# Linformer attention and a maxout feed-forward on one core: swapping the halves of odd head pairs, and an ln moved ahead

## The chip, the core and the metric

The kernel runs on one core of a Trainium2 chip. The metric is the device time in microseconds of one execution. The engines of the core are named here as in the profile: PE is TensorE (its matmuls; PEld is its loading of weights, the stationary operand), DVE is VectorE, ACT is ScalarE, POOL is GpSimd, SP is SyncE. Matmuls write to PSUM, which the program holds as one tile `ps` of 128 partitions by 8 banks of 512 float32.

## The reference

```python
batch, n_heads, seq, head_dim, k_proj = 8, 8, 1024, 64, 64
k_proj = einsum('ks,bhsd->bhkd', E, k)            # 1024 keys become 64
v_proj = einsum('ks,bhsd->bhkd', F, v)
scores = q @ k_proj.T / sqrt(64)                  # 1024 x 64 for each head
attn   = exp(scores - max) / (sum + 1e-9)
x      = (attn @ v_proj) as [8192 tokens, 512]    # heads side by side
h      = maximum(maximum(x @ w1, x @ w2), x @ w3) # 512 -> 768
out    = h @ w_out                                # 768 -> 512
```

The weights are random with a standard deviation of 1/sqrt(fan-in), q, k and v of 0.1. The kernel computes in bf16 with float32 sums, and leaves out the maximum in the softmax.

## The kernel before

A batch goes through two stages: attention, which ends in the transposed activations `xT`, and the feed-forward in two halves of 512 tokens (`ch`): layer 1 (18 groups of four matmuls, `l1`) and the output projection (`down`). The attention of batch b+1 is sewn into the feed-forward of batch b: `tick()` counts groups, and `at(slot, ...)` puts a piece of attention behind the group with that number. [...]

Batch 0 has nothing to hide behind and is written in a form of its own. Eight heads make four pairs `g`, and the two heads of a pair are its halves `u`. In the scores of batch 0 a pair holds its projected keys on 128 partitions, 64 for each half, and the probabilities `pT` also have one half on partitions 0 to 63 and the other on 64 to 127:

```python
HEAD = (0, 1, 2, 3, 5, 4, 7, 6)
QUADS = [(hh, j, HEAD[4 * hh + j] // 2, HEAD[4 * hh + j] % 2) for j in range(4) for hh in range(2)]
AB = 4
HD = D // 2
# ...
def quads0(ch, bank, lhs, hhs=(0, 1)):
    for hh, j, g, u in QUADS:
        if hh not in hhs:
            continue
        rows = slice(u * KP, (u + 1) * KP)
        nc.tensor.matmul(out=ps[j * HD:(j + 1) * HD, bank + hh, :], lhsT=lhs(rows, g),
                         rhs=pT[0][rows, g, ch, :], start=True, stop=True, tile_position=(u * KP, j * HD))
# ...
def v_proj0(g, bank):
    for si in range(SI):
        for u in range(2):
            nc.tensor.matmul(out=ps[u * KP:(u + 1) * KP, bank, g * D:(g + 1) * D], lhsT=fT[:, si, :],
                             rhs=v_t[0][:, HEAD[2 * g + u], si, :], start=(si == 0), stop=(si == SI - 1))
    nc.vector.tensor_copy(out=vp2[0][:, g], in_=ps[:, bank, g * D:(g + 1) * D].rearrange("p (dd f) -> p f dd", f=2))

def scores0(ch, g, bank):
    for u in range(2):
        rows = slice(u * D, (u + 1) * D)
        nc.tensor.matmul(out=ps[u * KP:(u + 1) * KP, bank, :], lhsT=kpT[0][rows, g, 0, :],
                         rhs=qT[0][rows, 4 * ch + g, :], start=True, stop=True)
# ...
def scores_up0():                       # the second half of batch 0's tokens
    for g, bank in ((0, 4), (1, 5), (2, 6), (3, 7)):
        scores0(1, g, bank)
    for g in (0, 2):
        nc.scalar.activation(out=pT[0][:, g:g + 2, 1, :], in_=ps[:, 4 + g:6 + g, :], func=AF.Exp, scale=scale)
```

`quads0` serves for the sums (with ones as weights) and for the AV product (with the projected v): eight matmuls of 64 rows by 32 columns, in eight tiles of the array. A score matmul contracts 64 rows into 64 columns, so the array has four tiles for it: row half by column half. In the first half of the tokens the scores of the four pairs have other matmuls between them (`k_proj0`, `q_turn0`, warm-ups); only `scores_up0` has the four pairs one after the other.

For the later batches, sums, ln, reciprocal and AV are:

```python
def sums(b):
    for ch in range(2):
        quads(b, ch, AB + 2 * ch, lambda rows, g: ones[rows, :])
    log(0)

def log(ch):
    nc.scalar.activation(out=lns[ch], in_=ps[:, AB + 2 * ch:AB + 2 * ch + 2, :], func=AF.Ln)

def recip(ch):
    nc.scalar.activation(out=rinv[ch], in_=lns[ch], func=AF.Exp, scale=-1.0)
# ...
def norm(b, f, ch, bank):
    nc.vector.tensor_tensor(out=xT[b % 2][:, f::2, ch, :], in0=ps[:, bank:bank + 2, :],
                            in1=rinv[ch].rearrange("p (u n) -> p u n", u=2), op=ALU.mult)

def av3(b):
    lo = fpair()                        # a free pair of banks 0 to 3
    for f, ch, bank in ((0, 0, lo), (1, 0, AB), (0, 1, AB + 2)):
        av(b, f, ch, bank)
    norm(b, 0, 0, lo)
```

Each `av` is a set of eight matmuls as in `quads0`. The first of the three in `av3` goes to a pair of the feed-forward's banks, the second over the sums of the first half (banks 4, 5), the third over the sums of the second half (6, 7).

Where batch 1's attention lies in batch 0's feed-forward, and the same pieces of batch 2 in batch 1's:

```python
if b == 0:
    at(9, scores_up0)
    at(12, sums0, 1, 4)
    at(19, kv, 1)                       # projections of batch 1, need its k and v
    # ...
    at(27, scores, 1, 0)
    at(30, scores, 1, 1)
    at(33, sums, 1)
    at(34, recip, 0)
    at(35, log, 1)
    at(35, av3, 1)
    at(36, recip, 1)
    at(36, norm, 1, 1, 0, AB)
    at(38, norm, 1, 0, 1, AB + 2)
elif b == 1:
    at(2, kv, 2)
    # ...
    at(15, av1, 1)
    at(15, sums, 2)
    at(15, log, 1)
    at(16, recip, 0)
    at(18, recip, 1)
    # ...
    at(25, av3, 2)
```

`down(b, ch, c, tt)`, the output projection of 128 tokens, is six matmuls and a copy by ScalarE to `o_acc`; four of them end batch 0.

Of the kernel before, what the change touches and what calls it, by code (L numbers as in the profile page):

```python
# [16 lines left out]
def kernel(ctx: ExitStack, tc: tile.TileContext, q, k, v, E, F, w1, w2, w3, w_out, out):  # L17
    nc = tc.nc
    B, H, S, D = q.shape
    KP = E.shape[0]  # L20
# [11 lines left out]
    def T(shape, dt, name):  # L32
        return sb.tile(shape, dt, name=name)

    ps = pp.tile([P, 8, 512], FP32, name="ps")
# [6 lines left out]
    fT = T([P, SI, KP], BF16, "fT")  # L42
# [9 lines left out]
    kpT = [T([P, H, 2, KP], BF16, f"kpT{i}") for i in range(NB)]  # L52
    vp2 = [T([P, NPAIR, 2, D // 2], BF16, f"vp2_{i}") for i in range(3)]
    pT = [T([P, NPAIR, 2, 512], BF16, f"pT{i}") for i in range(2)]
# [59 lines left out]
    HD = D // 2  # L114

    def kv(b, bank=AB):
        i = b % NB
        for si in range(SI):
            nc.tensor.matmul(out=ps[0:KP, bank, :], lhsT=eT[:, si, :], rhs=k_t[i][:, :, si, :],  # L119
                             start=(si == 0), stop=(si == SI - 1))  # L120
            nc.tensor.matmul(out=ps[KP:P, bank, :], lhsT=fT[:, si, :], rhs=v_t[i][:, :, si, :],  # L121
                             start=(si == 0), stop=(si == SI - 1))
        kp_ = kp2[i].rearrange("k h f r dd -> k (h f) r dd")
        kv_v = ps[KP:P, bank, :].rearrange("p (g u dd f) -> p u g f dd", u=2, f=2, dd=HD)
        nc.scalar.copy(out=kp2[i][:, :, :, 0, :], in_=ps[0:KP, bank, :].rearrange("p (h dd f) -> p h f dd", dd=HD, f=2))  # L125
        nc.scalar.copy(out=vp2[b % 3][KP:P], in_=kv_v[:, 1])
        nc.vector.tensor_copy(out=kp_[:, :, 1:], in_=kp_[:, :, 0:1].to_broadcast([KP, 2 * H, 3, HD]))
        nc.vector.tensor_copy(out=vp2[b % 3][0:KP], in_=kv_v[:, 0])
        nc.sync.dma_start_transpose(out=kpT[i].rearrange("p h f k -> p (h f) k"),
                                    in_=kp2[i].rearrange("k h f r dd -> k (h f r dd)"))  # L130
# [60 lines left out]
    def fbank():  # L191
        ring.append(ring.pop(0))
        return ring[-1]
# [57 lines left out]
                nc.gpsimd.dma_start(out=out_0[0][:, tt - 1:tt + 1, :], in_=o_acc[0][:, tt - 1:tt + 1, :])  # L251


    def quads0(ch, bank, lhs, hhs=(0, 1)):
        for hh, j, g, u in QUADS:
            if hh not in hhs:
                continue
            rows = slice(u * KP, (u + 1) * KP)
            nc.tensor.matmul(out=ps[j * HD:(j + 1) * HD, bank + hh, :], lhsT=lhs(rows, g),  # L259
                             rhs=pT[0][rows, g, ch, :], start=True, stop=True, tile_position=(u * KP, j * HD))  # L260

    def k_proj0(g):
        for si in range(SI):
# [5 lines left out]
    def v_proj0(g, bank):  # L269
        for si in range(SI):  # L270
            for u in range(2):
                nc.tensor.matmul(out=ps[u * KP:(u + 1) * KP, bank, g * D:(g + 1) * D], lhsT=fT[:, si, :],
                                 rhs=v_t[0][:, HEAD[2 * g + u], si, :], start=(si == 0), stop=(si == SI - 1))
        nc.vector.tensor_copy(out=vp2[0][:, g], in_=ps[:, bank, g * D:(g + 1) * D].rearrange("p (dd f) -> p f dd", f=2))

    def scores0(ch, g, bank):
        for u in range(2):
            rows = slice(u * D, (u + 1) * D)
            nc.tensor.matmul(out=ps[u * KP:(u + 1) * KP, bank, :], lhsT=kpT[0][rows, g, 0, :],  # L279
                             rhs=qT[0][rows, 4 * ch + g, :], start=True, stop=True)  # L280

    def exp0(ch, g, bank):
# [36 lines left out]
    def av_up0():  # L319
        for f, bank in enumerate((6, 4)):  # L320
            quads0(1, bank, lambda rows, g: vp2[0][rows, g, f, :])
        norm0(1, 0, 6, (0, 1))
        norm0(1, 1, 4, (0, 1))
# [40 lines left out]
    for y, dst in enumerate((eT, fT)):  # L364
        for si in range(SI):
            for x in range(2):
                nc.tensor.matmul(out=ps[x * D:(x + 1) * D, y, si * KP:(si + 1) * KP], lhsT=ef_b[:, y, si::SI],
                                 rhs=ident[:, x::2], start=True, stop=True)
# [51 lines left out]
    def l1_first(i, jts, banks, between=None):  # L420
        for hh in range(2):
            if hh and between:
                between()
            for jt, bank in zip(jts, banks):
                for ct in (2 * hh, 2 * hh + 1):
                    nc.tensor.matmul(out=ps[:, bank, :], lhsT=w_sb[i][:, ct, jt * P:(jt + 1) * P], rhs=xT[0][:, ct, 0, :],  # L426
                                     start=(ct == 0), stop=(ct == NCT - 1))
                if hh:
                    nc.vector.tensor_tensor(out=h1c[jt] if i == 1 else hT[0][:, jt, :], in0=ps[:, bank, :], in1=h1c[jt],  # L429
                                            op=ALU.max)  # L430
                    yield
# [7 lines left out]
    load(1, v, v_t)  # L439
    load(1, q, q_t)  # L440
    v_proj0(0, 3)
    warmup(1, 2)
    sums_part0(1)
    warmup(4, 2)
    v_proj0(1, 3)
    warmup(1, 2)
    av0(0, 0)
    av0(1, 0)
    norm0(0, 0, 6, (0,))
    norm0(0, 1, 7, (0,))  # L450
    v_proj0(2, 3)
    warmup(1, 2)
    w1_ct(0)
# [13 lines left out]
    for b in range(B):  # L467
        n = b + 1
        groups = []

        def at(slot, f, *args):
            groups.append((slot, lambda: f(*args)))
# [4 lines that stand above are left out]
            at(19, kv, 1)  # L477
            for g, x in enumerate((21, 22, 24, 25)):
                at(x, q_flip, 1, g)
            at(22, load_behind_turn, 2, "kvq")  # L480
            at(27, scores, 1, 0)
            at(30, scores, 1, 1)
            at(33, sums, 1)
            at(34, recip, 0)
            at(35, log, 1)
            at(35, av3, 1)
            at(36, recip, 1)
            at(36, norm, 1, 1, 0, AB)
# [3 lines that stand above are left out]
            for g in range(4):  # L492
                at(4 + g, q_flip, 2, g)
            at(9, load_behind_turn, 3, "kvq")
            at(8, scores, 2, 0)
            at(12, scores, 2, 1)
# [5 lines that stand above are left out]
            at(24, load, 4, k, k_t)  # L502
            at(24, load, 4, v, v_t)
            at(25, av3, 2)
            at(26, norm, 2, 1, 0, AB)
            at(28, norm, 2, 0, 1, AB + 2)
            at(30, kv, 3)
            for g in range(4):
                at(32 + 2 * g, q_flip, 3, g)
        elif n < B:  # L510
            if b + 2 < B:
                at(3, lambda: kv(b + 2, fbank()))
            at(3, scores, n, 0)
            at(8, scores, n, 1)
            if b + 3 < B:
                at(11, load_behind_turn, b + 3, "qkv", 4 if b == 2 else None)
            at(14, av1, b)
            at(14, sums, n)
            at(14, log, 1)
            at(15, recip, 0)  # L520
            at(17, recip, 1)
            at(26, av3, n)
            at(27, norm, n, 1, 0, AB)
            at(29, norm, n, 0, 1, AB + 2)
            if b + 2 < B:
                for g in range(4):
                    at(33 + 2 * g, q_flip, b + 2, g)
        else:
            at(5, av1, b)
        slot = 0  # L530
        gi = 0

        def tick():
            nonlocal slot, gi
            slot += 1
            while gi < len(groups) and groups[gi][0] <= slot:
                groups[gi][1]()
                gi += 1

        for ch in range(2):  # L540
            c = 2 * b + ch
            if c == 0:
                for part in ((1, range(6), (6, 7, 0, 1, 4, 5)), (2, range(3), (2, 3, 0), q_up0), (2, range(3, 6), (1, 2, 3))):
                    for _ in l1_first(*part):
                        tick()
                ring[:] = [0, 1, 2, 3]
                for x in range(2):
                    if x:
                        av_up0()
                    for tt in range(4):  # L550
                        down_half(tt, x)
                        if x:
                            tick()
                continue
            for s in range(18):
                l1(b, ch, c, s // 3, s % 3)
                tick()
                if pend and s in (2, 5, 8, 11):
                    pend.pop(0)()
                    tick()  # L560
            pend = [lambda tt=tt, b=b, ch=ch, c=c: down(b, ch, c, tt) for tt in range(4)]
        if b == 0:
            while pend:
                pend.pop(0)()
                tick()
# [32 lines left out]
```

The softmax here doesn't subtract the row's maximum and nothing guards it: scores larger than these inputs give would overflow.

## Time and profile before

The device time is 397.1 us, the median of three runs (397.05 to 397.64). The profiled execution has a span of 395.6 us.

| | busy us | share of the span | instructions |
|---|---|---|---|
| TensorE matmuls | 385.5 | 97% | 2691 |
| TensorE weight loads | 173.6 | 44% | 2742 |
| VectorE | 201.0 | 51% | 296 |
| ScalarE | 162.7 | 41% | 247 |
| GpSimd | 66.5 | 17% | 109 |

How to read what follows: a timeline line has the start in us from the span's start, the length in us of what is merged in it, the engine, the line of the kernel, the operation, what it writes and reads, the shape, and how many instructions it holds (x8). In brackets at its end stands how long the engine was idle before it, and what released it. Matmuls are pipelined, and the end of one is modelled; starts are the safer figure. Some matmul records can be missing. A group of the page has busy time, mean ns of one instruction, and idle time before it. "The chain" is followed back from the last instruction, at each step to what released it.

Line numbers are those of the kernel before: L259 is the matmul in `quads0`, L279 in `scores0`, L155 in `quads` (sums and AV of the later batches), L141 in the later batches' scores, L119 and L121 in `kv`, L164 is ln, L167 the reciprocal, L173 the normalization, L208 layer 1, L233 and L235 `down`'s matmul and copy, L426 and L246 layer 1 and output projection of batch 0's first half, L87 the loads of q, k and v.

### The profile page before, as it was taken

Reading aid. Unit: us, or ns where it says so; the run is one execution under the profiler, and the core shown is the slowest. Engines: PE = TensorE matmul, PEld = TensorE weight load, DVE = VectorE, ACT = ScalarE, POOL = GpSimd, SP = SyncE. Lnnn points to the kernel's source line nnn. Section 1 sums busy time; section 2 is a strip of 40 time slices with the busy share of each in tenths; the row PEclk is TensorE's granted clock in tenths of the full one; section 3 lists DMA queues with packets and bytes.
Section 4 is the critical chain, followed back from the end, with each engine's and each line's share of the span. In section 5 each row is a group of like instructions: output and inputs, shape, how many; then the busy total and the mean of one; then the engine's idle time right before and its main releaser. Section 6 shows DMA issues by size and latency. Waiting matters only on the chain.

```text
span 395.6 us, 6594 instructions
## 1 busy us (share of the span) xinstructions
PE 385.5 (97%) x2691; PEld 173.6 (44%) x2742; DVE 201.0 (51%) x296; ACT 162.7 (41%) x247; POOL 66.5 (17%) x109
## 2 busy tenths in 40 slices
PE   8999998999999999999999999999999999999996
PEld 4444443444444444444444444444444444444443
DVE  3347375555662476435764347625664456443342
ACT  4414446465326613356224632266234452222221
POOL 7452131162002501050000500000010000000000
PEclk9999999999999999999999999999999999999999
DMA  8999979979953995169711893121011111101023
GB/s 224 206 209 206 205 178 202 224 117 205 206 139 81 174 206 168 42 119 204 180 56 28 152 205 123 55 59 64 13 53 55 53 56 53 56 36 70 2 106 106
DMA packets 41437, 48.39 MB, mean 122 GB/s; under 512 B 9152, under 2 KB 36544, under 8 KB 41408
## 3 DMA queue, kind: packets, MB, share of 16 engines
q0 software_dynamic: 31776, 43.52, 53.0%
q1 hardware_dynamic: 8656, 3.41, 4.6%
q10 hardware_dynamic: 976, 1.05, 0.8%
q8 instruction: 21, 0.34, 0.3%
q14 instruction: 8, 0.07, 0.0%
HBM read 57.15 MB, written 16.78 MB: 187 GB/s over the span
## 4 chain that ended last, share of the span: by engine, by line
PE 92%; DMA 5%; issue 1%; DVE 1%; ACT 0%; POOL 0%; POOLq 0%; DVEq 0%
PE ps L208 59%; PE ps L233 19%; PE ps L119 3%; PE ps L155 3%; DMA w_sb<-in_moe_w_dram 3%; PE ps L426 2%; PE ps L141 2%; DMA k_t<-in_k_dram 2%; PE ps L246 1%; PE ps L417 1%; PE ps L226 1%; PE ps L259 0%; DVE h1s L429 0%; DVE o_acc L429 0%; PE ps L279 0%
## 5 line engine op out<-in xcount | busy, mean ns | idle before, releaser
L208 PE MATMUL ps<-xT,w_sb 128*128 128x512 bf16 x1049 | 242.9, 379 | 1.7
L208 PEld LDWEIGHTS <-w_sb 128*128 128x128 bf16 x1080 | 103.6, 98 | 130.0 <-issue 8.6
L213 DVE TENSOR_TENSOR m<-ps,h1s 128x512 f32<-128x512 f32 x90 | 62.2, 691 | 131.5 <-PE ps L208 99.1
L233 PE MATMUL ps<-wo_sb,hT 128*128 128x512 bf16 x335 | 82.3, 379 | 0.5 <-issue 0.2
L211 ACT COPY h1s<-ps 128x512 f32<-128x512 f32 x90 | 53.0, 589 | 67.4 <-PE ps L208 67.0
L235 ACT COPY o_acc<-ps 128x512 f32<-128x512 f32 x58 | 34.0, 587 | 102.3 <-PE ps L233 86.8
L215 DVE TENSOR_TENSOR hT<-ps,m 128x512 bf16<-128x512 f32 x90 | 62.0, 689 | 10.2 <-PE ps L208 2.4
L240 POOL DMA_DIRECT2D out_dram<-o_acc x28 | 15.2, 543 | 265.9 <-ACT o_acc L235 263.7
L233 PEld LDWEIGHTS <-hT 128*128 128x128 bf16 x348 | 33.5, 98 | 41.2 <-issue 1.7
L173 DVE TENSOR_TENSOR xT<-ps,rinv 128x1024 bf16<-128x1024 f32 x28 | 33.5, 1218 | 10.0 <-PE ps L155 7.8
L146 ACT ACTIVATE pT<-ps 128x1024 bf16<-128x1024 f32 x28 | 27.1, 1021 | 6.5 <-PE ps L141 6.2
L101 DVE STREAM_TRANSPOSE qT<-q_t 128x512 f32<-128x512 f32 x28 | 18.6, 689 | 0.0
L87 POOL DMA_DIRECT2D v_t<-in_v_dram x21 | 15.3, 747 | 11.1 <-PE ps L208 4.7
L164 ACT ACTIVATE lns<-ps 128x1024 f32<-128x1024 f32 x14 | 13.7, 1022 | 5.8 <-PE ps L155 5.8
L167 ACT ACTIVATE rinv<-lns 128x1024 f32<-128x1024 f32 x14 | 14.8, 1062 | 0.0
L121 PE MATMUL ps<-v_t,fT 128*64 128x512 bf16 x56 | 13.4, 382 | 0.0
L119 PE MATMUL ps<-k_t,eT 128*64 128x512 bf16 x56 | 13.4, 382 | 0.0
L125 ACT CAST kp<-ps 64x512 bf16<-64x512 f32 x7 | 4.1, 579 | 18.5 <-PE ps L121 18.5
L87 POOL DMA_DIRECT2D k_t<-in_k_dram x14 | 10.6, 769 | 2.3 <-ACT o_acc L464 1.1
L87 POOL DMA_DIRECT2D q_t<-in_q_dram x14 | 10.6, 773 | 2.0 <-DMA wo_sb<-in_moe_w_out_dram 1.1
L426 PE MATMUL ps<-xT,w_sb 128*128 128x512 bf16 x46 | 10.6, 379 | 0.2 <-issue 0.2
L155 PE MATMUL ps<-pT,vp 64*32 64x512 bf16 x224 | 8.9, 381 | 1.8 <-ACT lns L164 1.0
(84 smaller groups left out, 159.2 us busy)
## 6 DMA issues: line engine op xcount, KB each, us to landing
out_dram<-o_acc POOLq DMA_DIRECT2D x30, 512.0 KB, 3.0
q_t<-in_q_dram POOLq DMA_DIRECT2D x15, 512.0 KB, 12.1
k_t<-in_k_dram POOLq DMA_DIRECT2D x14, 512.0 KB, 12.1
v_t<-in_v_dram POOLq DMA_DIRECT2D x18, 256.0 KB, 14.5
v_t<-in_v_dram POOLq DMA_DIRECT2D x7, 512.0 KB, 14.1
w_sb<-in_moe_w_dram POOLq DMA_DIRECT2D x4, 384.0 KB, 10.3
k_t<-in_k_dram POOLq DMA_DIRECT2D x4, 256.0 KB, 7.9
w_sb<-in_moe_w_dram POOLq DMA_DIRECT2D x4, 192.0 KB, 10.1
```

What stands on the lines that cost most here:

```text
L87: nc.gpsimd.dma_start(out=dst[b % NB][:, slots], in_=sv[:, heads])
L101: nc.vector.transpose(out=qT[b % NB][:, hs].bitcast(FP32).rearrange("p h n -> p (h n)"), in_=q_t[b % NB][:, hs].rearrange("p h si d -> p ( ...
L119: nc.tensor.matmul(out=ps[0:KP, bank, :], lhsT=eT[:, si, :], rhs=k_t[i][:, :, si, :], start=(si == 0), stop=(si == SI - 1))
L146: nc.scalar.activation(out=pT[i][:, 2 * u + gg].rearrange("p ch (t r n) -> p r (ch t) n", t=4, r=4), in_=ps[:, AB:AB + 4, gg * 256:(gg + 1 ...
L155: nc.tensor.matmul(out=ps[j * HD:(j + 1) * HD, bank + hh, :], lhsT=lhs(rows, g), rhs=pT[b % NB][rows, g, ch, :], start=True, stop=True, ti ...
L173: nc.vector.tensor_tensor(out=xT[b % 2][:, f::2, ch, :], in0=ps[:, bank:bank + 2, :], in1=rinv[ch].rearrange("p (u n) -> p u n", u=2), op= ...
L208: nc.tensor.matmul(out=ps[:, bank, :], lhsT=w_sb[i][:, ct, jt * P:(jt + 1) * P], rhs=xT[b % 2][:, ct, ch, :], start=(ct == 0), stop=(ct == ...
L211: nc.scalar.copy(out=h1s[jt % 2], in_=ps[:, bank, :])
L213: nc.vector.tensor_tensor(out=m12[jt % 2], in0=ps[:, bank, :], in1=h1s[jt % 2], op=ALU.max)
L215: nc.vector.tensor_tensor(out=hT[c % 2][:, jt, :], in0=ps[:, bank, :], in1=m12[jt % 2], op=ALU.max)
L233: nc.tensor.matmul(out=ps[:, bank, :], lhsT=hT[c % 2][:, jt, tt * P:(tt + 1) * P], rhs=wo_sb[:, jt, :], start=(jt == 0), stop=(jt == NJT - 1))
L235: nc.scalar.copy(out=o[:, tt, :], in_=ps[:, bank, :])
```

## The change

In batch 0 the halves of the odd pairs change places wherever they lie along the keys' axis: in the scores' output, in the projected v, and in what the sums and the AV product read. An even pair's scores then go from rows 0 to 63 to columns 0 to 63 and from rows 64 to 127 to columns 64 to 127 of the array, as before; an odd pair's go from the upper rows to the lower columns and the other way round. It is meant to let two pairs run side by side in all four 64x64 tiles. Apart from that, the second ln of batch 1 is put behind the first, ahead of the reciprocal and of the AV units that write over its sums. The number of instructions is the same on all engines, and so are the loads.

```diff
+    def half(g, u):
+        x = u ^ (g % 2)
+        return slice(x * KP, (x + 1) * KP)
+
     def quads0(ch, bank, lhs, hhs=(0, 1)):
         for hh, j, g, u in QUADS:
             if hh not in hhs:
                 continue
-            rows = slice(u * KP, (u + 1) * KP)
+            rows = half(g, u)
             nc.tensor.matmul(out=ps[j * HD:(j + 1) * HD, bank + hh, :], lhsT=lhs(rows, g),
-                             rhs=pT[0][rows, g, ch, :], start=True, stop=True, tile_position=(u * KP, j * HD))
+                             rhs=pT[0][rows, g, ch, :], start=True, stop=True, tile_position=(rows.start, j * HD))
 # ...
     def v_proj0(g, bank):
         for si in range(SI):
             for u in range(2):
-                nc.tensor.matmul(out=ps[u * KP:(u + 1) * KP, bank, g * D:(g + 1) * D], lhsT=fT[:, si, :],
+                nc.tensor.matmul(out=ps[half(g, u), bank, g * D:(g + 1) * D], lhsT=fT[:, si, :],
 # ...
     def scores0(ch, g, bank):
         for u in range(2):
             rows = slice(u * D, (u + 1) * D)
-            nc.tensor.matmul(out=ps[u * KP:(u + 1) * KP, bank, :], lhsT=kpT[0][rows, g, 0, :],
+            nc.tensor.matmul(out=ps[half(g, u), bank, :], lhsT=kpT[0][rows, g, 0, :],
                              rhs=qT[0][rows, 4 * ch + g, :], start=True, stop=True)
 # ...
             at(33, sums, 1)
+            at(33, log, 1)
             at(34, recip, 0)
-            at(35, log, 1)
             at(35, av3, 1)
```

## The prediction

> **What bounds the kernel now.** I read the page first: the engine totals, the slices and the chain that ended last.
>
> ```profile
> PE 385.5 (97%) x2691; PEld 173.6 (44%) x2742; DVE 201.0 (51%) x296; ACT 162.7 (41%) x247; POOL 66.5 (17%) x109
> ...
> PEclk9999999999999999999999999999999999999999
> ...
> PE 92%; DMA 5%; issue 1%; DVE 1%; ACT 0%; POOL 0%; POOLq 0%; DVEq 0%
> ```
>
> TensorE is busy 97% of a 395.6 us span at full granted clock, and 92% of the chain is its own work. So only two things shorten the run: less TensorE time, or an idle moment of TensorE taken away. The change offers one of each, and each is found in a narrow timeline.
>
> Part A is the upper half of batch 0's scores. These are TensorE's matmuls, then its weight load of what follows:
>
> ```profile
> 34.36 1.05 PE L279 MATMUL ps<-qT,kpT 64*64 64x512 bf16 x8
> 35.57 0.59 PE L426 MATMUL ps<-xT,w_sb 128*128 128x512 bf16 x2 [0.16 <-issue]
> ...
> 35.34 0.55 PEld L426 LDWEIGHTS <-w_sb 128*128 128x128 bf16 x4 [0.41 <-issue]
> ```
>
> Looked at in still narrower windows, the eight matmuls start two by two: at 34.36, 34.60, 34.82 and 35.04, some 0.22 us apart. That is four rounds of two. The last two starts are 0.30 us ahead of the next weight load at 35.34. The "0.16 issue" in front of the matmul at 35.57 isn't to be believed: the whole group has 12 weight loads (x12 at 35.34) and 11 matmul records (x11), so the first matmul's record is missing, and it ran with its load at 35.34. From the first score to the next block is therefore 35.34 - 34.36 = 0.98 us.
>
> Other small matmuls of the same kernel, in 64x32 tiles, show what more tiles at once give:
>
> ```profile
> 38.04 0.41 PE L259 MATMUL ps<-pT,ones 64*32 64x512 bf16 x8
> 38.38 0.39 PE L246 MATMUL ps<-wo_sb,hT 128*128 128x512 bf16 x1
> ...
> 41.08 0.63 PE L259 MATMUL ps<-pT,vp 64*32 64x512 bf16 x16
> 41.63 0.39 PE L246 MATMUL ps<-wo_sb,hT 128*128 128x512 bf16 x1
> ```
>
> Eight matmuls in eight tiles take 0.34 us until the next block starts; sixteen, two rounds, take 0.55. One round more costs 0.21.
>
> Part B is the end of batch 0, where batch 1's AV units run. TensorE and its weight load, then ScalarE:
>
> ```profile
> 65.17 0.62 PE L155 MATMUL ps<-pT,vp 64*32 64x512 bf16 x16
> 66.84 0.41 PE L155 MATMUL ps<-pT,vp 64*32 64x512 bf16 x8 [1.04 <-ACT lns L164]
> 67.17 0.33 PEld L233 LDWEIGHTS <-hT 128*128 128x128 bf16 x3 [0.23 <-issue]
> ...
> 62.83 1.02 ACT L164 ACTIVATE lns<-ps 128x1024 f32<-128x1024 f32 x1 [0.61 <-PE ps L155]
> 63.89 1.06 ACT L167 ACTIVATE rinv<-lns 128x1024 f32<-128x1024 f32 x1
> 65.28 0.59 ACT L235 COPY o_acc<-ps 128x512 f32<-128x512 f32 x1 [0.33 <-PE ps L233]
> 65.76 1.03 ACT L164 ACTIVATE lns<-ps 128x1024 f32<-128x1024 f32 x1
> ```
>
> The third AV unit writes the two banks that held the sums of the second half, so it has to wait until the second ln has read them. ScalarE does that ln fourth, after a reciprocal and a copy, although the sums were there at about 62.9. TensorE stands for 1.04 us. The same three units in batch 1, where both ln come before them:
>
> ```profile
> 97.47 0.84 PE L155 MATMUL ps<-pT,vp 64*32 64x512 bf16 x24
> 98.24 1.04 PE L233 MATMUL ps<-wo_sb,hT 128*128 128x512 bf16 x4
> ```
>
> **What the Trainium skill says.** "TensorE: Matmul & The Clock Gate", in "Part 3: Packing small matmuls — row/col tiling", says that matmuls in different tiles of the array run at the same time and start a few ns apart. The trace agrees: the pairs above start 3 ns apart. "TensorEngine Tiling (Array Packing)", "Restrictions and Gotchas", says that row tiles may not write one PSUM bank at the same moment. "PSUM — Partial Sum Buffer", in "PSUM bank collisions raise a hardware error", narrows that to the same quadrant of 32 partitions within a bank. The new layout keeps to it: even pairs fill the diagonal tiles, odd pairs the other two, and the two matmuls of one column half write different banks. "Perfetto Trace Analysis", "Tensor Engine Instruction (MATMUL, LD_WEIGHTS)", says that ScalarE is strictly first in, first out. That is what part B turns on, and the order above, with an ln behind a copy that itself waited 0.33 us, agrees.
>
> **The change part by part.**
>
> A. Nothing is added: the eight score matmuls are the same, but pairs 0 and 1 (then 2 and 3) now use four different 64x64 tiles. I count two rounds of four instead of four of two. Two rounds to the next block is the 0.55 us of the sixteen above, against 0.98: 0.43 us less. The start of batch 0 also calls the score function, but there other matmuls stand between the pairs, so nothing can overlap. The exp that follows (35.02 to 36.96) may start some 0.2 us earlier, and the sums that need it come at 38.04 - 0.43 = 37.61, still after it. Before the next block's second bank is free, VectorE must have finished its maximum, which runs from 34.21 to about 34.9; TensorE will want that bank at 34.91 + 0.43 = 35.34. So no new wait here.
>
> B. ScalarE's order becomes ln 0, ln 1, reciprocal 0, copy, copy, reciprocal 1. From the durations above, ln 1 ends about 62.83 + 2 x 1.02 = 64.87 at the latest, before AV starts at 65.17. The 24 matmuls then run in one piece as in batch 1: 98.24 - 97.47 = 0.77 us to the next block, where it now takes 67.17 - 65.17 = 2.00 us. That is 1.23 us less. Of it 1.04 is the wait shown; the rest is a pipeline that needn't start twice. (Here too I use the weight load at 67.17: 18 loads and 17 matmuls are recorded.)
>
> What B delays: reciprocal 0 ends about 65.93 instead of 64.95. The normalization on VectorE starts now at 65.72, so 0.2 us later; its two steps take 2.36 us and end near 68.3. The next layer-1 matmuls need them about 71.0 - 1.2 = 69.8. The copy of the first output tile ends about 66.5 instead of 65.9, and its bank is wanted by the third down block at about 65.94 + 1.29 = 67.2. Both have room.
>
> Sum: 0.43 + 1.23 = 1.66 us at most, if everything behind is TensorE's own. I checked what else has a date of its own. Batch 1's projection starts at 46.92, and v for it comes late:
>
> ```profile
> 31.16 0.72 POOL L87 DMA_DIRECT2D v_t<-in_v_dram  x1 [1.97 <-DMA q_t<-in_q_dram]
> ...
> v_t<-in_v_dram POOLq DMA_DIRECT2D x1, 256.0 KB, 15.3
> ...
> 46.92 0.40 PE L121 MATMUL ps<-v_t,fT 128*64 128x512 bf16 x1
> ```
>
> 31.16 + 15.3 is a landing near 46.5, and the DMA engines are full until about 53 us, so that date doesn't move with TensorE. After part A the projection would be ready at 46.49. That is exactly on the date; I take 0.07 us off for it. Batch 1's turned k lands at 55.13 (issue at 50.10, 5.0 us), its scores start at 55.78 - 0.36 = 55.42: room of 0.3. Batch 2's v lands about 69.1 for a projection at 72.89 - 1.6 = 71.3: room of 2. Later loads are earlier still against their use. So 1.6 us, of 397.1: 395.5.
>
> **Rivals.** First, v's date eats part A: if in an unprofiled run it lands 0.3 us later than in this one, A yields about 0.1, and the time is 395.8. For it: the near coincidence. Against: the kernel before shows no wait there at all.
>
> Second, four tiles don't run four at a time, say because two column halves can't take different moving data from the same rows. Then A is nothing and the time is 395.9. Against: the 64x32 matmuls above do this in eight tiles, and batch 1's scores put 32 matmuls of 256 columns into 0.59 us.
>
> Third, ScalarE's new order makes a wait elsewhere: a later reciprocal 0 holds up normalization, layer 1 and a bank. I put the room at 0.7 us or more; if it were none, B would keep about 0.9 and the time would be 395.8.
>
> Fourth, the swapped row order of the sums and AV units at the start (rows 0, 64, 64, 0 instead of alternating) costs a round. Until 20.8 us the chain is a weight transfer (10.27 to 20.50), which hides it; behind it a single pair of units is exposed, 0.2 us. The full sets already have neighbours on the same rows and run in one round, so I give this little.
>
> **Range and chances.** The best case is 397.1 - 1.7 = 395.4; with a run-to-run spread of 0.6 us in the three times before, 394.9 is the low end. If only B holds, and loses a few tenths, it is 396.2. Two per cent would be 7.9 us, almost five times what both parts hold, and nothing that is added could cost so much. So within 2% at 0.985, the rest for surprises.
>
> **What would show it.** The score line should read x8 with about 0.62 us instead of 1.05, and the next weight load come about 0.55 after it starts. On ScalarE the two ln should stand together near 62.4, before the first reciprocal; batch 1's AV should be one line of x24 with 0.84, without a wait for the ln. At the projection of batch 1 a wait for v of at most 0.1 us may appear; a longer one would speak for the first rival. The gap between the two traces should be 0.4 us at 36 us, 0.35 at 49 us, 1.6 at 70 us, and stay there. If it shrinks after 72 us, something with a date of its own has taken it back, and my reading of the later stages is wrong.

## The result

The changed kernel takes 395.85 us, the median of six runs (395.35 to 396.22), against 397.1 us in as many runs of the kernel before (397.05 to 397.92). The ratio is 0.9963, with a 95% interval of 0.995 to 0.9976: 1.5 us less by the ratio, with 1.0 to 2.0 in the interval; by the medians it is 1.25. The prediction was 395.5, in a range of 394.9 to 396.2.

The page of the kernel after, the same lines as were shown of the one before (in the second, of the chain, the order of the small shares differs):

```profile
PE 384.6 (98%) x2691; PEld 173.5 (44%) x2742; DVE 201.0 (51%) x296; ACT 162.5 (41%) x247; POOL 66.5 (17%) x109
...
PE 91%; DMA 6%; issue 1%; POOL 0%; ACT 0%; DVE 0%; POOLq 0%
```

TensorE is busier as a share of a span of 394.4 us, and a transfer has gained a place in the chain: the turned k of batch 2, below. From here on, lines of the kernel beyond `quads0` stand five further down: L279 has become L284, L426 L431.

Part A in the timeline after, matmuls and then weight loads:

```profile
34.05 0.63 PE L284 MATMUL ps<-qT,kpT 64*64 64x512 bf16 x8
34.83 2.54 PE L431 MATMUL ps<-xT,w_sb 128*128 128x512 bf16 x11 [0.16 <-issue]
...
34.60 1.41 PEld L431 LDWEIGHTS <-w_sb 128*128 128x128 bf16 x8 [0.41 <-issue]
```

From the first score to the next block's weight load it is 34.60 - 34.05 = 0.55 us, where it was 0.98. That is the predicted 0.43 us. The gap before the matmul at 34.83 is again a missing record: 12 matmuls are issued there and 11 recorded.

Part B: TensorE with its weight loads, then ScalarE, then VectorE:

```profile
64.46 0.84 PE L155 MATMUL ps<-pT,vp 64*32 64x512 bf16 x24
...
65.23 0.76 PEld L233 LDWEIGHTS <-hT 128*128 128x128 bf16 x5 [0.42 <-issue]
...
62.12 1.94 ACT L164 ACTIVATE lns<-ps 128x1024 f32<-128x1024 f32 x2 [0.61 <-PE ps L155]
63.95 1.06 ACT L167 ACTIVATE rinv<-lns 128x1024 f32<-128x1024 f32 x1
64.89 0.59 ACT L235 COPY o_acc<-ps 128x512 f32<-128x512 f32 x1
...
65.04 2.35 DVE L173 TENSOR_TENSOR xT<-ps,rinv 128x1024 bf16<-128x1024 f32 x2 [1.07 <-ACT rinv L167]
```

Both ln are through at 62.12 + 1.94 = 64.06, before the AV units start, and the 24 matmuls are one piece: 65.23 - 64.46 = 0.77 us instead of 2.00. Normalization now waits for the reciprocal, and no wait for normalization shows.

Then a part of it is lost. These are batch 2's first scores after and before, and the transfer that turns their k, which ScalarE's and VectorE's copies release. In this last view the number is the time from issue to landing:

```profile
79.76 0.66 PE L141 MATMUL ps<-qT,kpT 32*64 32x256 bf16 x32 [0.75 <-DMA kpT<-kp]
...
kpT<-kp SPq DMA_TRANSPOSE x1, 5.6
```

```profile
80.89 0.66 PE L141 MATMUL ps<-qT,kpT 32*64 32x256 bf16 x32
...
kpT<-kp SPq DMA_TRANSPOSE x1, 3.5
```

The turned k was issued at 74.12 instead of 76.07, and landed at 79.72 instead of 79.57. Set side by side, weight load by weight load, the kernel after is ahead by 0.31 us when it reaches the changed scores (the start of the two profiled runs differed by that), by 0.74 behind them, by 1.95 behind batch 1's AV units, and by only 1.13 from batch 2's scores to the end: 0.82 us lost on the turned k.

### The profile page after: what moved, and what is told of

It is laid out like the page before. It is cut to its first block, busy times and chain, and to the rows that moved or that the text cites. A ratio compares the mean times of both kernels' runs of the same rounds, so it can differ in the third digit from the quotient of the medians.

```text
span 394.4 us, 6594 instructions
## 1 busy us (share of the span) xinstructions
PE 384.6 (98%) x2691; PEld 173.5 (44%) x2742; DVE 201.0 (51%) x296; ACT 162.5 (41%) x247; POOL 66.5 (17%) x109
## 4 chain that ended last, share of the span: by engine, by line
PE 91%; DMA 6%; issue 1%; POOL 0%; ACT 0%; DVE 0%; POOLq 0%
PE ps L208 58%; PE ps L233 19%; PE ps L119 3%; PE ps L155 3%; PE ps L431 3%; DMA w_sb<-in_moe_w_dram 2%; PE ps L141 2%; DMA k_t<-in_k_dram 2%; DMA kpT<-kp 1%; PE ps L246 1%; PE ps L422 1%; PE ps L226 1%; PE ps L264 0%; PE ps L311 0%; POOL k_t L347 0%
## 5 line engine op out<-in xcount | busy, mean ns | idle before, releaser
L431 PE MATMUL ps<-xT,w_sb 128*128 128x512 bf16 x46 | 10.6, 379 | 0.2 <-issue 0.2
L127 DVE COPY kp<-kp 64x1536 bf16<-64x1536 bf16 x7 | 3.9, 552 | 12.4 <-ACT kp L125 12.4
```

## Experiments

The theory: A is worth 0.43 us, B 1.23, and what is missing is taken by a transfer with a date of its own. The rivals: a part is worth less away from the profile, or the late k was a single odd transfer. Leads are in us against the profiled kernel before, taken between the weight loads of both traces.

**Each part alone.** With the second ln back in its old place, and with the kernel before with that ln moved:

```diff
-            at(33, log, 1)
             at(34, recip, 0)
+            at(35, log, 1)
             at(35, av3, 1)
```

> The changed kernel with the second ln of batch 1 back where it was: part A alone. Theory (two rounds of four tiles, and batch 2's turned k has a date of its own): the eight score matmuls read 0.62 us instead of 1.05, 0.43 us are gained and pass to the end, because batch 2's scores then come at about 80.5 us and their k has landed by about 79.6: 396.7 us. Rival (the score matmuls gain nothing off the profile, the start is only scattered): 397.1.

> The kernel before with both ln ahead of batch 1's AV units: part B alone. Theory: AV runs as one line of 24 and TensorE gains 1.23 us at 67 us; batch 2's scores then come at about 79.6 us, just when their turned k lands, so 0 to 0.5 us are lost there: 395.9 to 396.4 us. Rival (nothing is taken back at batch 2's k): the whole 1.23, 395.9, and no wait of the score's weight loads for a transfer.

Part A alone: 397.0 us (21 runs) beside 397.33 of the kernel before (27 runs), ratio 0.999, interval 0.9984 to 0.9997. Part B alone: 396.01 us, ratio 0.9968, interval 0.9956 to 0.9979. As ratios these are 0.4 and 1.27 us, against 0.43 and 1.23 expected; together 1.67. In their traces the scores of A read x8 with 0.63 us, and B gains 1.23 between 66 and 69 us. B alone had no wait for k: it landed at 79.31, and the scores came at 79.58. In its profile A keeps 0.31 of its 0.43 us to the end, as 0.13 goes at batch 1's v (below), and B keeps all. The 1.67 agrees with the sum of 1.66, but the intervals are wide: 0.1 to 0.6 us for A, 0.8 to 1.7 for B.

**The changed kernel again**, three times: once beside these two (the second profile), then twice on another chip (the third, and the fourth beside the last three kernels below).

> The changed kernel again, for a second profile. Theory (batch 2's turned k lands when the loads and stores beside it are through, whatever TensorE does): k lands between 78.4 and 79.8 us although it is issued near 74.1, and the scores, ready at 78.9, wait 0 to 0.9 us; the time scatters with that between 395.4 and 396.3. Rival (the 0.8 us wait of the first profile was one odd transfer): landing near 77.7, 3.5 us after issue as in the kernel before, no wait, and 395.4 us throughout.

> The changed kernel once more, for a third profile. Theory: batch 2's turned k lands 0.95 us after the second store of batch 0's second half, wherever in 77.7 to 78.8 us that falls, and the scores wait for it only if that is above 79.2. Rival: the landing is tied to its issue, 3.5 us later, 77.9.

> The changed kernel, to stand beside the next three on one chip. Theory: batch 2's turned k lands 0.95 us after the second store of batch 0's second half; the scores wait for it whenever that is later than some 79 us in a trace without a late start; device time 1.2 to 1.6 us below the kernel before on the same chip.

With the second profile stand 395.9 us, ratio 0.9962 (0.9949 to 0.9974); k landed at 79.06, and the scores at 79.21 did not wait. With the fourth stand 396.18 us, ratio 0.9968 (0.9956 to 0.998), k at 78.52, no wait. The third, a single execution, took 397.13 where the kernel before had a median of 397.75, and its wait is longer than in any other:

```profile
80.70 0.55 PE L141 MATMUL ps<-qT,kpT 32*64 32x256 bf16 x24 [1.04 <-DMA kpT<-kp]
...
kpT<-kp SPq DMA_TRANSPOSE x1, 5.9
```

Its second store landed at 79.71, outside what I had expected for stores, and k 0.95 us behind it. Taken together (transfers ahead of k are the two stores of batch 0's second half, but q where these are not there; wait is beyond the usual 0.42 us before scores):

| kernel | last transfer ahead landed | k issued | k landed | scores start | wait |
|---|---|---|---|---|---|
| before | 77.51 | 76.07 | 79.57 | 80.89 | none |
| A alone | 77.63 | 75.64 | 79.20 | 80.46 | none |
| B alone | 78.35 | 74.76 | 79.31 | 79.58 | none |
| changed, first profile | 78.81 | 74.12 | 79.72 | 79.76 | 0.82 |
| changed, second | 78.11 | 74.39 | 79.06 | 79.21 | none |
| changed, third | 79.71 | 74.77 | 80.66 | 80.70 | 1.11 |
| changed, fourth | 77.61 | 74.57 | 78.52 | 79.39 | none |
| without the stores | 75.54 | 74.36 | 77.91 | 79.19 | none |
| stores behind k | 75.17 | 74.50 | 78.02 | 79.32 | none |

In all nine rows k lands either about 3.5 us after its issue or 0.9 to 1.0 us after the last transfer ahead of it, whichever is later; the five profiles that are not in the table fit too. In the kernel before the first of these ended last; in the changed kernel, with k issued 1.3 to 2 us earlier, the second does.

**Without the two stores.** 512 rows of the output stay unwritten.

```diff
-        elif tt % 2 == 1:
+        elif tt % 2 == 1 and c != 1:
```

> The changed kernel without the two output stores of batch 0's second half (512 rows of the output stay unwritten), which are issued near 68 and 70 us, ahead of batch 2's turned k. Theory (the turned k is through 3.5 us after its issue, or 0.95 us after the last transfer ahead of it, whichever is later): last load near 75.5, issue near 74.4, landing near 77.9 us, well before the scores need it at 79.2. Rival (its time is its own, and the later landings of the changed kernel are scatter): 78.7 to 79.8 as with the stores.

The last q landed at 75.54, k at 77.91, 3.5 us after its issue; the one execution took 395.61 us. This is its line, with the share of busy DMA engines from 74 to 78 us in 40 slices:

```profile
DMA  1121111111000002899999999999999961000000
...
kpT<-kp SPq DMA_TRANSPOSE x1, 3.5
```

The kernel after, from 74 to 80 us:

```profile
DMA  9999999999999979999111111101119996000000
```

The digit 1 for a good microsecond, just before the last burst, says that some two of sixteen engines were still at work on what came earlier. Packet by packet, 456 of the turned k's 1024 packets had ended by 76.8 us, the next one ended at 77.98, and most of the rest came in the last burst, after the last packet of the loads and stores at 78.37. So the turned k is held by what was issued ahead of it. Why that ends up to 2 us earlier or later from run to run was not tried.

**Batch 1's v.** Twelve matmuls that stand before batch 1's projection are left out: the first half of the contraction in the output projection of batch 0's first 512 tokens, whose outputs lack it.

```diff
-                                 rhs=wo_sb[:, jt, :], start=(jt == 0), stop=(jt == NJT - 1))
+                                 rhs=wo_sb[:, jt, :], start=(jt == 3), stop=(jt == NJT - 1))
 # ...
-                    for tt in range(4):
+                    for tt in range(4) if x else ():
                         down_half(tt, x)
```

> The changed kernel without the first half of the contraction in the output projection of batch 0's first 512 tokens: twelve matmuls of TensorE fewer at 38 us (these outputs lack that half), some 1.3 us or more off TensorE's way to batch 1's projection, after what the AV units then wait for ln. Theory (batch 1's v has a date of its own at 46.4 us, and part A had just used up the room before it): the projection waits for v some 1.2 us and starts within 0.1 us of the changed kernel's; the time is 395.8, under 0.2 below the changed kernel. Rival (v is simply in time): 394.5 us.

395.75 us, ratio 0.9956, interval 0.9939 to 0.9972, which holds the changed kernel's ratio; the rival's 394.5, a ratio of 0.992, lies outside it. The changed kernel ran only once beside it, at 397.13 with a k wait of 1.11 us that this profile hasn't, so the trace has to show where the saved time went. Beside the changed kernel's second profile the lead is 2.1 us just ahead of the projection and 0.17 behind it, and v itself landed 0.17 us earlier here. The projection in this trace, and in that of the kernel after:

```profile
44.32 0.40 PE L119 MATMUL ps<-k_t,eT 128*64 128x512 bf16 x1
46.33 0.38 PE L121 MATMUL ps<-v_t,fT 128*64 128x512 bf16 x1 [1.60 <-issue]
```

```profile
46.18 0.40 PE L119 MATMUL ps<-k_t,eT 128*64 128x512 bf16 x1
46.24 0.38 PE L121 MATMUL ps<-v_t,fT 128*64 128x512 bf16 x1
```

The k part starts at once and the v part 2.0 us later, after v landed at 46.24. The profile names this wait "issue"; only the landing tells what it was. I had put what is saved ahead of it at 1.3 us, and it was about 2; the rest is as the theory says. In the kernel after, v landed at 46.15, the two parts are 0.06 us apart, and the lead falls by 0.03.

**Order of the pairs.**

```diff
-        for g, bank in ((0, 4), (1, 5), (2, 6), (3, 7)):
+        for g, bank in ((0, 4), (2, 6), (1, 5), (3, 7)):
```

> The changed kernel with the four pairs of the upper scores issued as 0, 2, 1, 3, so that neighbours share their two tiles. Theory (a matmul waits only for the one before it in its own tile, and starts keep program order): three rounds, pair 0, then 2 with 1, then 3; from the first score to the next block's weight load 0.34 + 2 x 0.21 = 0.77 us, between the 0.55 of the changed kernel and the 0.98 of the kernel before. Rival (it isn't the tiles, but something else in the new layout): 0.55 as in the changed kernel.

Here matmuls, weight loads and ScalarE's first exp:

```profile
34.95 0.63 PE L284 MATMUL ps<-qT,kpT 64*64 64x512 bf16 x8
...
35.52 0.76 PEld L431 LDWEIGHTS <-w_sb 128*128 128x128 bf16 x5 [0.41 <-issue]
...
35.63 1.02 ACT L322 ACTIVATE pT<-ps 128x1024 bf16<-128x1024 f32 x1 [1.41 <-PE ps L284]
```

0.57 us, not 0.77. Starts are four near 34.96 and four near 35.20, two rounds. Pairs 0 and 2 have the same two tiles and can't share a round, so in the first must have been pair 0 with 1 or 3: a matmul that stands behind a waiting one got past it. My three rounds fall. The rival explains the number but not the mechanism: layouts before and after differ in tiles and in nothing else that touches the scores. Its time, 397.16 in a single execution, holds an 0.88 us wait for k, which landed at 80.67.

**Two ways to get the k wait out.** Batch 2's scores and sums two groups later, tried twice, and the two stores behind the turned k. A further kernel has the stores behind and batch 1's projection one group later.

```diff
-            at(8, scores, 2, 0)
-            at(12, scores, 2, 1)
+            at(11, scores, 2, 0)
+            at(14, scores, 2, 1)
             at(15, av1, 1)
-            at(15, sums, 2)
-            at(15, log, 1)
-            at(16, recip, 0)
-            at(18, recip, 1)
+            at(17, sums, 2)
+            at(17, log, 1)
+            at(18, recip, 0)
+            at(20, recip, 1)
```

```diff
         nc.gpsimd.tensor_copy(out=seen, in_=kpT[(b - 1) % NB][:, 0, 0, 0:1])
+        if b == 3:
+            for tt in (1, 3):
+                nc.gpsimd.dma_start(out=out_0[1][:, tt - 1:tt + 1, :], in_=o_acc[1][:, tt - 1:tt + 1, :])
 # ...
-        elif tt % 2 == 1:
+        elif tt % 2 == 1 and c != 1:
 # and in the further kernel
-            at(19, kv, 1)
+            at(20, kv, 1)
```

> The changed kernel with batch 2's scores, sums, ln and reciprocals two groups (about 1.7 us of layer 1) later in batch 1. Theory: batch 2's turned k is always there when the scores come, no wait of TensorE, the whole gain of 1.66 us passes: 395.4 us, about 0.4 below the changed kernel, and less scatter. Rival (the wait is not what holds the changed kernel above 395.4): the same as the changed kernel, 395.85; or worse, if the later sums make the reciprocals late for the AV units eight groups on.

> The changed kernel with batch 2's scores, sums, ln and reciprocals two groups later, again, beside the others on one chip. Theory: no wait for the turned k either, so the same as with the stores behind. Rival (the first comparison holds everywhere): the same as the changed kernel.

> The changed kernel with the two output stores of batch 0's second half issued behind batch 2's turned k, ahead of batch 3's loads; the output is complete. Theory: k lands 3.5 us after its issue, or 0.95 us after the last load of q if that is later (75.5 to 77.1 so far), so before the scores need it; no wait of TensorE, 0 to 1.1 us less than the changed kernel on this chip. Rival (the wait moves on: batch 3's loads start with 1 MB of stores before them, 2.5 us later): a wait at batch 3's projection near 102 us, or none at all and the same time as the changed kernel.

> As the one before, and batch 1's projection one group (0.86 us of layer 1) later. Theory: v has landed when the projection comes, so the 0.06 to 0.18 us that it took from part A are saved; its turned k still lands only 0.9 us after the stores at 54.2, near 55.1, and the scores at 55.2 just don't wait: 0.1 us below the one before, too little to be told apart by time. Rival (the turned k comes later with its later issue): 0.3 to 0.6 us above the one before, with a wait of the first scores near 55.

| kernel | us | ratio to before | interval |
|---|---|---|---|
| changed, beside the first | 395.9 | 0.9962 | 0.9949 to 0.9974 |
| scores later | 395.96 | 0.9967 | 0.9955 to 0.998 |
| changed, beside the next three | 396.18 | 0.9968 | 0.9956 to 0.998 |
| scores later, again | 396.09 | 0.997 | 0.9959 to 0.9982 |
| stores behind | 395.74 | 0.9964 | 0.9951 to 0.9976 |
| stores behind, projection later | 395.79 | 0.9963 | 0.9951 to 0.9976 |

None is told apart from the changed kernel: the intervals lie over each other. In these two groups the profile of the changed kernel had no k wait to take out, so the comparison says little about the runs that have one. The later scores miss their 395.4 in part for a reason that the trace shows: batch 1's last AV unit and batch 2's sums, 24 matmuls with 0.77 us to the next block when together, stand apart there and take 0.34 + 0.55 = 0.89. The lead falls by 0.17 us between 87 and 107 us, and 0.31 went at batch 1's v; the 395.4 was also reckoned from 397.1, where the kernel before took 397.33 beside them. With the stores behind, k lands at 78.02, with over a microsecond of room, and no wait turns up at batch 3's projection. That is sound, but shown only in its trace, not in its time. The further kernel did as expected, k of batch 1 landing at 55.23 and v costing nothing (a lead of 0.34 us on both sides of the projection), and nothing is gained that time would show.

## Why the prediction was right, and where not

**Part A, 0.43 us**: right, 0.98 to 0.55 in the trace, and 0.4 us (0.1 to 0.6) as a run of its own. The argument from the 64x32 matmuls held. The rival that column halves can't work at once on different data from the same rows is out.

**Part B, 1.23 us**: right, 2.00 to 0.77 in the trace, 1.27 us as a run of its own. The delays were harmless, as worked out.

**v's date**: right in kind; the 0.07 us was one case of several. v took 0.03 us in the first profile of the changed kernel, 0.06 in the second and nothing in the last two, 0.13 with A alone, and 0.31 in that of the first kernel with later scores, where a lead of 0.76 shrank to 0.45. And with 2 us more taken out of TensorE ahead of it, nothing was gained. Part A used what room there was.

**"Later loads are earlier still against their use"** is the step that failed. I had gone through v of batches 1 and 2 and batch 1's turned k, but not batch 2's turned k, which in the kernel before came 80.89 - 79.57 = 1.3 us ahead of its scores. With its issue 1.95 us earlier that would be safe if landing followed issue by 3.5 us. It doesn't: it also has to wait for the transfers ahead, and these ended at 77.61 to 79.71 us in the changed kernel against 77.51 before, though the two stores among them were issued earlier too (in the first profile 67.62 and 70.21 instead of 69.56 and 72.15). Batch 2's v, which had been given a room of 2 us, landed later too, in the first profile at 70.28 instead of 69.07; its projection came at 70.95, so the room was down to 0.67. The sign that the prediction had named for this came true in the first profile, where the lead was as forecast up to 70 us (0.43 and 1.64 beyond the 0.31 of the start) and then shrank by 0.82. The sum of 1.66 us is thus an upper figure, off which came 0, 0, 0.82 and 1.11 us in four profiles of the changed kernel. Whether that is all of the distance between 395.85 and 395.5 the runs can't say; it is as large as their scatter. That the median lies in the range is partly luck: the range's upper end came from other causes, and the execution with the wait of 1.11 us took 397.13, outside it, though 0.36 us of that was lost at the start.

**Start of batch 0** with its swapped rows: no cost seen behind 20.5 us, where the rival put it: from there to the changed scores no profile's lead changes by more than 0.03 us. Ahead of that, the profiles scatter too much to tell: at the changed scores the four of the changed kernel stand from 0.31 us ahead to 0.36 behind, and that of the other order of pairs 0.59 behind.

## What to carry to other kernels

When work ahead of a wait is removed, list every transfer that is awaited later, with two dates: one that moves with its issue, and one that is set by what is in the queues ahead of it. The room is the distance to the later of both, not the distance seen in the profile. And put an instruction that frees a buffer ahead of those that only prepare the next step: on ScalarE here, an ln two places earlier was worth three times as much as four tiles at work instead of two.

## What was not expected

With the pairs in the order 0, 2, 1, 3 the scores still took two rounds. The Trainium skill, "TensorE: Matmul & The Clock Gate", in "Part 3: Packing small matmuls — row/col tiling", says that matmuls start and end strictly in program order. Eight starts in two groups of four, with the first two pairs in the same two tiles, don't fit that: a matmul whose tile is busy did not hold up the one behind it with a free tile. ScalarE's first exp, which needs pairs 0 and 1, started 0.68 us after the first score in place of 0.46 in the changed kernel, which is one round later. The trace also has the semaphores of each instruction, and they say more. The fifth start, at 35.19, is the matmul that waits for VectorE's copy of q, which pairs 2 and 3 need (signalled at 34.90, ahead of the first score); so pair 2 opened the second round. The fourth, at 34.97, is one of the two that signal ScalarE. In the changed kernel these two signals came 0.43 and 0.40 us after the starts of their matmuls; here they came at 35.61 and 35.65, and the first is 0.64 us after its start, behind the second round. So the starts left program order while the signals of the ends kept to it, and ScalarE gained nothing from the matmul that got ahead. This is one execution.
